# Packed attention and a squared-ReLU MLP on one core: two more banks offered to the folded weights and the second scores, and a new table for the planner

## The chip, the core and the metric

The kernel runs on one core of a Trainium2 chip. TensorE (PE in the profile) multiplies matrices out of SBUF into PSUM, the accumulation memory; PSUM has eight banks, numbered 0 to 7 here, and one bank holds 512 float32 numbers in each of 128 partitions. VectorE (DVE) and ScalarE (ACT) read results from PSUM and write SBUF. GpSimd (POOL) and SyncE (SP) mostly issue DMAs. PEld is TensorE's loading of the stationary operand, which the profile lists as an engine of its own.

The metric is the time of one execution on the device, in microseconds (us); lower is better.

## The reference, cut to what matters

```python
def sm_attn(qq, kk, vv):                       # per batch and head
    a = softmax(qq @ kk.T / 8)
    return a @ vv
p_packed = sm_attn(p, k, v)                    # 32 packed rows
x = sm_attn(q, p_packed, p_packed)             # 576 tokens
h = x.reshape(4608, 512) @ w_in                # heads side by side; w_in is 512 x 2048
out = square(relu(h)) @ w_out                  # w_out is 2048 x 512
```

There are 8 batches of 8 heads, 576 tokens and 64 numbers per head. `x` has 8 x 576 = 4608 rows.

## The kernel before, in words

The work goes batch by batch, eight heads as two "quads" of four. For each batch b, with the names that the code gives to the pieces of work:

- **S1** (L736, for batches 5 to 7 L752): first scores, packed rows times keys. MX (L755) takes the maximum, EX (L763, on ACT) the exponential. E (L769) transposes the exponentials on TensorE, EC copies them out of PSUM (L609 on ACT or L611 on DVE); for batches 5 to 7 a DMA transposes instead.
- **PV** (L783): the packed values. XN (L792) normalizes them, XQ (L796) and XM (L802) turn them, XC copies XM's result.
- **M** (L813, four pieces c of eight matmuls): the *folded weights*. The packed values are multiplied into `w_in`, so that the second attention's probabilities can be multiplied by the result at once and `x` is never formed. A piece fills two banks; MC (L609 or L611) evicts it to SBUF.
- **S2** (L830, for batches 5 to 7 L840): the *second scores*, queries times packed values. A piece of batches 0 to 4 fills part of two banks; SI (L851) takes it out with a transpose, and then follow on DVE and ACT the softmax's maximum (L857), subtraction (L861), exponential (L864, ACT), sum and reciprocal (L867, L868), product (L874) and a transposition into the tile `a` (L878). Batch 0 does this in three parts of 128, 192 and 256 tokens, batch 1 in two of 256 and 320, the others in one.
- **F** (L915 for batches 0 and 1, L887 for the others): hidden layer from `M` and `a`, into two banks; R (L923 or L925, L897 or L899) is the ReLU, Q (L933 or L935, L905 or L907) the square, written into `gT`.
- **Output**: tiles of 128 tokens times `w_out`, F2 (L941). Tiles in the groups of batches 2 to 7 are done instead in pieces GP (L1008) from sums and differences of quarters of `gT` and `w_out` (GS, L993; WS, L986), which saves one product of eight; GC (L1028) adds the pieces up. FZ (L959) is one tile done in two halves. Stores go out on SP, ACT and POOL.

**What sets the order.** No engine's order is written out by hand. `kernel_impl` describes every piece of work to a `Plan` (L47) with `add`: its engine or a choice of engines with a duration for each, the pieces it depends on, a level, and what it takes. `Plan.forward` (L70) is a list scheduler. It walks through its own model of time, and at each step lets go the ready piece of the lowest rank. The rank is the level plus a number from `TABLE` (the dictionary "o", 837 entries), and a second dictionary ("l", 584 entries) leans pieces that have a choice towards ACT or away from it. `run` (L199) then emits the instructions in the order of the planned starts. So every instruction's place on its queue and the choice of ACT or DVE come from the table. Where the plan leaves TensorE idle for long before the first F2, `fills` (L213) puts in idle matmuls (`keep_clock`, L613, on bank 7; L615 in the profile).

**PSUM in the plan.** A piece that writes PSUM names what it takes as a list of alternatives:

```python
PAIRS = [(0, 1), (2, 3), (4, 5)]
ONES = [(4,), (5,), (6,), (7,)]
OUTS = [(6,), (7,)]
RS = [(8 + i,) for i in range(NR)]
```

M, S2, F and S1 take from `PAIRS`, one pair or two. E and PV take from `ONES`. F2 takes from `ONES` (the first tiles) or `OUTS`, and GP and FZ from `OUTS`. `units` (L103) goes through the alternatives in their order and takes the first that is free in the plan; when none is free, the piece isn't ready. A pair is free again when the piece that evicts it is done. The last two banks, 6 and 7, were in `OUTS` and `ONES` alone. The dependencies between instructions that the chip waits for are made afterwards, when the pieces are emitted, from what the instructions read and write.

Of the kernel before, what the change touches and what calls it, by code (L numbers as in the profile page):

```python
# [14 lines left out]
P = 128  # L15
# [26 lines left out]
class Plan:  # L42
# [185 lines left out]
TABLE = {'o': {'Lk.0.0i': -36.900503, 'Lk.0.1i': 0.41924, 'Lk.0.0': -16.56608, 'LP.0': 169.009326, 'Lk.0.1':  # L228
# [292 lines left out]
def kernel_impl(tc, q, k, v, p, w_in, w_out, out):  # L521
# [23 lines left out]
    with ExitStack() as ctx:  # L545
# [42 lines left out]
        M = many("M", 2, [P, NQD, DFF], BF16)  # L588
# [532 lines left out]
        def lasts(b):  # L1121
            if b in PARTS:
                return [f"F.{b}.{x}.{NFB // parts(b)[x][1] - 1}" for x in range(len(parts(b)))]
            return [f"F1.{b}.{NFB - 1}"]
# [275 lines left out]
```

## Time and profile before

| | |
|---|---|
| median of 3 runs | 233.85 us (233.79 to 234.32) |
| the profiled execution | 233.42 us |
| its span, first to last instruction or DMA | 231.7 us |
| what lies around the span | 1.72 us |
| mean granted TensorE clock | 0.994 |
| DVE busy | 199.4 us (86%) |
| ACT busy | 148.4 us (64%) |
| POOL busy | 60.5 us (26%) |

The span counts from the first instruction. A view in stretches gives the busy time of each engine between two moments; the timeline gives instructions in order of time, joined where equal ones follow each other, with the idle time before them and what ended it in brackets; the chain of waits goes back from the last instruction through what released each step. A row "PE L887 MATMUL ... x20" covers twenty matmuls from the start of the first to the end of the last, and matmuls overlap: one lasts longer than the step from one to the next.

### The profile page before, as it was taken

How to read it: one execution, taken by the hardware profiler on the slowest of the kernel's cores; microseconds unless marked ns; L12 is line 12 of the kernel's file. 1: busy time of each engine (PE TensorE's matmuls, PEld its weight loads, DVE VectorE, ACT ScalarE, POOL GpSimd, SP SyncE). 2: the span in 40 equal slices, each digit the busy share in tenths (PEclk: the TensorE clock that was granted, in tenths of full speed). 3: DMA queues.
4: the chain of work that ended last, by engine and by line, in shares of the span. 5: the costliest groups of instructions: out<-in, count | busy, mean ns of one | idle time of the engine just before them, and what ended most of it. 6: DMA issues, size and time to landing. Idle time of an engine off the chain costs nothing.

```text
span 231.7 us, 6374 instructions
## 1 busy us (share of the span) xinstructions
PE 220.0 (95%) x2613; PEld 160.0 (69%) x2630; DVE 199.4 (86%) x336; ACT 148.4 (64%) x243; POOL 60.5 (26%) x108
## 2 busy tenths in 40 slices
PE   8978899999999999999999999999999999999991
PEld 5655664456654476768777877787668888888880
DVE  3679978999989999999999899999999997958340
ACT  3324994268955899775997936859988988310100
POOL 9787646333243575640000000000000000000010
PEclk9999999999999999999999999999999999999997
DMA  7999999999999999999999659757041001515325
GB/s 235 188 161 180 184 204 205 203 193 251 241 229 223 223 219 195 158 148 126 177 193 166 135 94 207 149 83 172 0 96 43 4 0 35 113 36 114 70 52 174
DMA packets 46668, 34.06 MB, mean 147 GB/s; under 512 B 25376, under 2 KB 38368, under 8 KB 46640
## 3 DMA queue, kind: packets, MB, share of 16 engines
q0 software_dynamic: 19488, 18.09, 50.5%
q1 hardware_dynamic: 26304, 14.98, 31.4%
q10 hardware_dynamic: 848, 0.59, 0.9%
q8 instruction: 20, 0.33, 0.6%
q14 instruction: 8, 0.07, 0.1%
HBM read 37.22 MB, written 9.44 MB: 201 GB/s over the span
## 4 chain that ended last, share of the span: by engine, by line
PE 83%; DVE 6%; DMA 5%; POOL 1%; issue 1%; ACT 1%; DVEq 0%; ACTq 0%; POOLq 0%
PE ps L1008 32%; PE ps L887 21%; PE ps L941 15%; PE ps L915 4%; PE ps L813 3%; DMA v_b<-in_v_dram 3%; DMA kq_b<-in_q_dram 2%; PE ps L959 2%; DVE gT L935 1%; PE ps L783 1%; PE ps L830 1%; PE ps L736 1%; PE ps L769 1%; POOL v_b L624 1%; DVE qT L700 1%
## 5 line engine op out<-in xcount | busy, mean ns | idle before, releaser
L897 ACT ACTIVATE r_b<-ps 128x576 bf16<-128x576 f32 x86 | 50.4, 663 | 10.1 <-PE ps L887 9.7
L887 PE MATMUL ps<-a,M 128*128 128x288 bf16 x384 | 52.3, 286 | 0.2 <-issue 0.2
L887 PEld LDWEIGHTS <-M 128*128 128x128 bf16 x384 | 37.3, 98 | 11.1 <-issue 0.2
L941 PE MATMUL ps<-w_out_b,gT 128*128 128x512 bf16 x159 | 41.3, 380 | 1.1 <-issue 0.6
L1008 PEld LDWEIGHTS <-gT 128*128 128x128 bf16 x384 | 36.9, 98 | 7.3 <-issue 1.3
L609 ACT CAST M<-ps 128x1024 bf16<-128x1024 f32 (+1 forms) x30 | 26.9, 933 | 12.4 <-PE ps L813 12.3
L609 ACT COPY o_sb<-ps 128x512 f32<-128x512 f32 (+1 forms) x23 | 12.9, 568 | 32.2 <-PE ps L1008 18.4
L1008 PEld LDWEIGHTS <-gS 128*128 128x128 bf16 x288 | 27.8, 98 | 4.5 <-issue 0.7
L953 POOL DMA_DIRECT2D out_dram<-o_sb x3 | 1.7, 556 | 108.8 <-ACT o_sb L609 103.6
L1028 DVE TENSOR_TENSOR o_sb<-o_sb,ps 128x512 f32<-128x512 f32 x30 | 20.3, 676 | 10.1 <-PE ps L1008 10.0
L907 DVE TENSOR_TENSOR gT<-r_b 128x1152 bf16<-128x1152 bf16 x37 | 27.1, 746 | 1.6 <-ACT r_b L897 1.6
L941 PEld LDWEIGHTS <-gT 128*128 128x128 bf16 x176 | 16.2, 98 | 15.4 <-issue 2.1
L1008 PE MATMUL ps<-wS,gT 128*128 128x256 bf16 x192 | 24.0, 273 | 0.0
L1008 PE MATMUL ps<-w_out_b,gT 128*128 128x256 bf16 x192 | 23.5, 273 | 0.0
L1008 PE MATMUL ps<-wS,gS 128*128 128x256 bf16 x192 | 23.3, 273 | 0.0
L923 ACT ACTIVATE r_b<-ps 128x512 bf16<-128x512 f32 (+2 forms) x30 | 17.8, 659 | 4.8 <-PE ps L915 4.7
L915 PE MATMUL ps<-a,M 128*128 128x256 bf16 (+3 forms) x160 | 18.3, 262 | 2.2 <-DVE a L878 1.0
L915 PEld LDWEIGHTS <-M 128*128 128x128 bf16 x160 | 14.0, 97 | 6.8 <-issue 2.2
L763 ACT ACTIVATE e<-ps,n 128x576 bf16<-128x576 f32 x16 | 11.7, 737 | 7.8 <-DVE n L755 7.6
L615 PE MATMUL ps<-o_sb 128*128 128x256 bf16 x89 | 13.9, 319 | 1.1 <-DVE o_sb L618 1.1
L755 DVE TENSOR_REDUCE n<-ps 128x1 f32<-128x576 f32 x16 | 11.6, 748 | 3.1 <-PE ps L736 3.0
L864 ACT ACTIVATE e<-s 128x1152 bf16<-128x1152 f32 (+4 forms) x11 | 10.0, 912 | 6.2 <-DVE s L861 6.1
(77 smaller groups left out, 322.0 us busy)
## 6 DMA issues: line engine op xcount, KB each, us to landing
out_dram<-o_sb SPq DMA_DIRECT2D x65, 128.0 KB, 3.5
kq_b<-in_k_dram POOLq DMA_DIRECT2D x14, 288.0 KB, 11.1
kq_b<-in_q_dram POOLq DMA_DIRECT2D x10, 288.0 KB, 8.7
w_in_b<-in_moe_w_in_dram POOLq DMA_DIRECT2D x16, 128.0 KB, 5.7
w_out_b<-in_moe_w_out_dram POOLq DMA_DIRECT2D x8, 256.0 KB, 9.6
v_b<-in_v_dram POOLq DMA_DIRECT2D x5, 320.0 KB, 11.8
v_b<-in_v_dram POOLq DMA_DIRECT2D x12, 128.0 KB, 8.7
v_b<-in_v_dram POOLq DMA_DIRECT2D x5, 256.0 KB, 12.2
```

The lines of the kernel that those rows point to most:

```text
L609: nc.scalar.copy(dst, src)
L615: nc.tensor.matmul(half(7)[:, :2 * P], lhsT=zero[:, :P], rhs=zero, start=True, stop=True)
L755: nc.vector.tensor_reduce(n1[b % 2][:, qd:qd + 1], ps1[b, qd], axis=AX.XY if b in XBAR else AX.X, op=ALU.max, negate=True)
L763: nc.scalar.activation(e_out(qd) if b in XBAR else e1[:, qd, :S], ps1[b, qd], ACT.Exp, bias=n1[b % 2][:, qd:qd + 1], accum_out=d1[b % 2][: ...
L887: nc.tensor.matmul(t[:, c], lhsT=M[b % 2][:, qd, fb * FB:(fb + 1) * FB], rhs=a2[b % 2][:, qd, c * HALF:(c + 1) * HALF], start=(qd == 0), s ...
L897: nc.scalar.activation(dst, src, ACT.Relu)
L907: eng.tensor_tensor(out=dst, in0=r, in1=r, op=ALU.mult)
L915: nc.tensor.matmul(t[:, c, m * w:(m + 1) * w], lhsT=M[b % 2][:, qd, fb * FB:(fb + 1) * FB], rhs=a2[b % 2][:, qd, o:o + w], start=(qd == 0) ...
L923: nc.scalar.activation(dst, ph["h", b, x, j], ACT.Relu)
L941: nc.tensor.matmul(po[t], lhsT=gT[:, fb, n0:n0 + P], rhs=w_out_b[:, fb, :], start=(fb == 0), stop=(fb == NFB - 1))
L1008: nc.tensor.matmul(pz[g, k][:, i], lhsT=a[:, f, i * P:(i + 1) * P], rhs=w[:, f], start=(k not in ON and h == 0 and f == 0 and i == 0), sto ...
L1028: nc.vector.tensor_tensor(out=oC(g, i, j), in0=oC(g, *src), in1=pz[g, z], op=ALU.add)
```

## The change

M's pieces and S2's pieces of batches 0 to 4 may also take banks 6 and 7 as a pair, the last alternative in their lists. The table is replaced: all 837 entries of "o" have new values, and "l" has 554 entries in place of 584. Nothing else is edited.

```diff
-TABLE = {'o': {'Lk.0.0i': -36.900503, 'Lk.0.1i': 0.41924, 'Lk.0.0': -16.56608, 'LP.0': 169.009326, 'Lk.0.1':
+TABLE = {'o': {'Lk.0.0i': -2.825591, 'Lk.0.1i': 2.561464, 'Lk.0.0': 25.82095, 'LP.0': 1.735445, 'Lk.0.1': 18.929428,
...
             for c in range(NWC):
                 add(f"M.{b}.{c}", [("PE", 0.216, lambda u, b=b, c=c: m_mm(b, c, u))], [f"XC.{b}"] + [f"LWI.{c}.{i}.{qd}" for i in range(2) for qd in QDS]
-                    + (lasts(b - 2) if b > 1 else []), line="M", take=[PAIRS], mode=3, level=L + 3)
+                    + (lasts(b - 2) if b > 1 else []), line="M", take=[PAIRS + [(6, 7)]], mode=3, level=L + 3)
...
-                add(f"S2.{b}.{x}", [("PE", 0.00088 * tok, lambda u, b=b, x=x: s2_mm(b, x, u))], [f"XQ.{b}"] + tq, line="S2", take=[PAIRS], mode=1, level=l2)
+                add(f"S2.{b}.{x}", [("PE", 0.00088 * tok, lambda u, b=b, x=x: s2_mm(b, x, u))], [f"XQ.{b}"] + tq, line="S2", take=[PAIRS + [(6, 7)]], mode=1, level=l2)
```

The new table is three lines shorter, so a line of the kernel after stands three lower than the same line before; line numbers here are those of the kernel before.

What the edit makes of the program can be read from the two lists of instructions, engine by engine:

| | before | after |
|---|---|---|
| matmuls, idle ones among them | 2632, 89 | 2630, 87 |
| changes of TensorE's tile shape from one matmul to the next, from the first 192-token F on | 64 | 68 |
| e evicted on DVE, on ACT | 7, 3 | 5, 5 |
| M evicted on DVE, on ACT, pieces of 1024 | 4, 24 | 2, 26 |
| ReLU of L887's results on DVE, on ACT | 10, 86 | 5, 91 |
| squares of these on DVE, on ACT | 37, 11 | 43, 5 |
| matmuls of M and S2 into banks 6 and 7 | 0 | 0 |

577 rows, old and new, of the table TABLE are left out of this document.

## The prediction

> **What bounds the kernel now.** I read the page's first part, then a view in five stretches, TensorE's own waits, and the chain of waits at its end.
>
> ```profile
> span 231.7 us, 6374 instructions
> PE 220.0 (95%) x2613; PEld 160.0 (69%) x2630; DVE 199.4 (86%) x336; ACT 148.4 (64%) x243; POOL 60.5 (26%) x108
> ```
> ```profile
> 0.00:23.53 23.53, 19.34 (x257) 13.20 (x258) 15.73 (x42) 8.69 (x16) 19.25 (x38) 1.00 1.07 190
> 23.53:31.43 7.90, 7.13 (x72) 5.62 (x71) 7.64 (x18) 7.71 (x15) 4.44 (x7) 1.00 1.18 192
> 31.43:63.55 32.12, 31.41 (x313) 17.87 (x318) 28.74 (x59) 21.28 (x39) 12.80 (x21) 1.00 1.21 217
> 63.55:197.81 134.26, 133.27 (x1711) 97.75 (x1723) 130.47 (x196) 107.43 (x170) 22.33 (x40) 1.00 0.80 134
> 197.81:231.70 33.89, 28.82 (x265) 25.57 (x262) 16.85 (x26) 3.30 (x7) 1.67 (x3) 0.96 0.37 90
> ```
> ```profile
> PE ps L915 <- DVE a L878: 1.0, 2, 0.6
> PE ps L915 <- ACT r_b L923: 0.5, 2, 0.3
> PE ps L915 <- DVE M L611: 0.3, 1, 0.3
> PE ps L736 <- DVE kT L703: 0.2, 1, 0.2
> ```
> ```profile
> 197.81 19.21 PE ps L1008 x176
> 224.89 1.76 PE ps L959 x16
> 226.67 0.37 ACT o_sb L609
> ```
>
> The stretches' columns are length, then PE, PEld, DVE, ACT and POOL busy, granted clock and DMA. From 31.43 to 197.81 TensorE is idle for 0.71 + 0.99 us out of 166, although DVE is nearly as full. In the last stretch it runs on to 226.65, and one eviction and the last store follow. So from 31.43 on the time is TensorE's amount of work, and an order can give back only what TensorE waits. The waits are early: of those listed, all but the 0.2 us on `kT` are before 31.43. In 23.53:31.43 ACT is busy for 7.71 of 7.90 us and DVE for 7.64: there the evictions are the bound.
>
> **The change part by part.**
>
> *The two banks.* In the new program's list of instructions no matmul of M (L813) or of the second scores (L830) writes bank 6 or 7, as in the old. Whenever the plan let such a piece go, one of the first three pairs was free. That edit costs and gives nothing, and no wait on these banks is added. What is left is the new order: TensorE's work is the same but for two idle matmuls fewer, and the choices of ACT or DVE that the table of the change counts.
>
> *The opening.* Up to the first 192-token F both lists have the same work on TensorE (idle matmuls apart). But both copies of the transposed exponentials (EC of batch 0), and one of ppT, move from DVE to ACT, where they stand between two exponentials.
>
> ```profile
> L609 ACT COPY e<-ps 128x640 bf16<-128x640 bf16 x3 | 2.1, 699 | 0.3 <-PE ps L769 0.3
> L611 DVE COPY e<-ps 128x640 bf16<-128x640 bf16 x7 | 3.3, 486 | 0.9 <-PE ps L769 0.7
> ```
> ```profile
> 9.93 0.45 PE L769 MATMUL ps<-ident,e 128*128 128x128 bf16 x5
> 10.84 0.74 ACT L763 ACTIVATE e<-ps,n 128x576 bf16<-128x576 f32 x1 [1.41 <-DVE n L755]
> 12.22 0.49 DVE L611 COPY e<-ps 128x640 bf16<-128x640 bf16 x1 [0.35 <-PE ps L769]
> 12.76 0.48 PE L783 MATMUL ps<-v_b,e 128*32 128x64 bf16 x40 [0.25 <-DMA w_in_b<-in_moe_w_in_dram]
> 16.48 0.65 DVE L700 STREAM_TRANSPOSE qT<-kq_b 128x448 f32<-128x448 f32 x1 [0.35 <-DMA kq_b<-in_q_dram]
> 23.10 0.38 DVE L878 STREAM_TRANSPOSE a<-n 128x192 f32<-128x192 f32 x1
> 23.53 2.69 PE L915 MATMUL ps<-a,M 128*128 128x192 bf16 x32 [0.64 <-DVE a L878]
> ```
>
> The first transpose ends at 10.38; ACT copies from 10.42 to 11.12, so the second exponential starts at 11.05 in place of 10.84 (+0.21), and its copy takes 0.699 in place of 0.486 (+0.21): PV starts 0.42 later, at 13.18, and so do the second scores. DVE has two copies less, though, and the new list puts a transposition of the queries ahead of the maximum. At 16.48 DVE waited 0.35 us for queries that come by DMA, in the same order in both lists. Laid end to end from PV, DVE gets there at 16.5: the delay is gone in that wait. The DVE work from there to `a` of the second part (L878 at 23.10) is the same set in a slightly better order: 23.0, and F starts at 23.45, 0.1 early. What hides the ACT copies is that 0.35 us; without it F comes about 0.4 late.
>
> *From 23.5 to the first scores of batch 1.*
>
> ```profile
> 26.89 1.08 PE L915 MATMUL ps<-a,M 128*128 128x256 bf16 x8 [0.29 <-ACT r_b L923]
> 28.26 1.91 PE L915 MATMUL ps<-a,M 128*128 128x256 bf16 x16 [0.28 <-DVE M L611]
> 30.00 0.49 PE L615 MATMUL ps<-o_sb 128*128 128x256 bf16 x3
> 30.69 0.60 PE L915 MATMUL ps<-a,M 128*128 128x256 bf16 x4 [0.19 <-ACT r_b L923]
> 31.43 0.70 PE L736 MATMUL ps<-kT,pT 32*32 32x512 bf16 x32
> ```
> ```profile
> L923 ACT ACTIVATE r_b<-ps 128x768 bf16<-128x768 f32 x4 | 3.0, 813 | 0.0
> L923 ACT ACTIVATE r_b<-ps 128x512 bf16<-128x512 f32 x18 | 10.0, 603 | 3.7 <-PE ps L915 3.6
> L933 ACT ACTIVATE gT<-r_b 128x512 bf16<-128x512 bf16 x8 | 4.7, 630 | 0.1
> ```
>
> The old order waits three times and puts in three idle matmuls. The new one mixes the parts (256, 128, 256, 192, 256 tokens in place of 28 matmuls of 256) and needs no idle ones. But every F piece takes a pair that a ReLU must free, and S1 takes two. ACT's list from the first wide ReLU, at 24.3, to the one that frees S1's second pair is three ReLUs of 768, four of 512, an M of 512 and squares of 768, 512 and 512: 2.44 + 2.41 + 0.6 + 0.87 + 1.26 = 7.6 us (0.87 is an estimate from the row of 512 by width), less 0.65 for ten overlaps, so to 31.25, and S1 starts there, 0.2 earlier than at 31.43. By then TensorE has done 2.84 us of F in place of 3.05, at 0.109 us per 256 columns (the chain's 19.21 for 176 matmuls of that width). Early by 0.2 with 0.2 more left is **0.0**. The bounds are -1.25 (the three waits, 0.76, and the idle matmuls, 0.49, all go) and +0.4 (the opening's cover fails).
>
> *More changes of tile shape.* From the first 192-token F on the new list changes the tile shape of TensorE 68 times in place of 64; all four are before the scores of batch 2, around M and S2.
>
> ```profile
> 95.22 0.77 PE ps L813 x24
> 95.99 3.60 PE ps L1008 x32
> 103.72 0.34 PE ps L813 x8
> ```
> ```profile
> L1008 PE MATMUL ps<-wS,gT 128*128 128x256 bf16 x192 | 24.0, 273 | 0.0
> ```
>
> In the chain of waits eight matmuls of L813 take 0.34 and 24 take 0.77, so each further eight cost 0.215, and 0.125 of the first 0.34 is the way in. The 32 of L1008 take 3.60 where 32 x 0.109 is 3.49: 0.11 on the way back. Four at 0.1 to 0.12 are **+0.4**, between 0 (the kinds differ, and some may be cheaper) and 0.5. The Trainium skill speaks against such an order: TensorEngine Tiling (Array Packing), Tiling Modes, Key Properties, says that changing the tiling mode drains the engine. If each drain cost the whole tail of a matmul, 0.273 us of duration less its 0.109 us step, four would be 0.66 by the page's rule; the rows here, 0.11 to 0.125, show less, and I take them.
>
> *F of batch 1 sooner.* The new list puts F of batch 1's first part after 25 output matmuls where the old has 36, and its third piece behind the transposition of the *second* part of `a` (the tile's parts overlap in address order, so it waits for it).
>
> ```profile
> 42.68 1.45 DVE L851 STREAM_TRANSPOSE s<-ps 128x512 f32<-128x512 f32 x2 [0.35 <-PE ps L830]
> 50.90 1.43 DVE L703 STREAM_TRANSPOSE kT<-kq_b 128x576 f32<-128x576 f32 x2
> 54.47 0.68 DVE L925 TENSOR_SCALAR r_b<-ps 128x512 bf16<-128x512 f32 x1
> 56.46 0.51 DVE L878 STREAM_TRANSPOSE a<-n 128x320 f32<-128x320 f32 x1
> 80.07 1.08 PE ps L941 x5
> ```
>
> From 42.68 to that transposition's end at 56.97 DVE spent 14.3 us. The new list has 3.2 us less in between (two `kT`, one ReLU in return for one eviction, one square, three weight sums at about 0.63, less stalls of 0.5 where steps now follow the one they need), and starts at about 41.7: ready at about 52.9. TensorE at its steps (0.216 for L941) arrives at 52.6: a wait of **+0.35**, between 0 and 0.8 (the 0.64 of 23.53 is the nearest row, and the chain may be 0.2 longer). Behind it stand all later matmuls.
>
> *Waits that go.* The 0.2 on `kT`, where the new order has ten transposes and thirteen output matmuls between the scores of batches 2 and 3, and perhaps 0.1 ahead of the former: **-0.3**, between -0.4 and 0. Later DVE and ACT have about 1 us less work each by the counts, and no wait of TensorE on them is seen in the old; I put 0 there, up to +0.5 as each of the listed single waits is 0.2 to 0.6. The end is unchanged: the same last tile, eviction and store.
>
> The sum is 0.0 + 0.4 + 0.35 - 0.3 = **+0.45**: a span of 232.15. With the 1.72 us that the profiled execution has around its span (233.42 - 231.7) it is 233.87, and as that execution was 0.43 below the median of 233.85, a median of **234.3**.
>
> **The rivals.**
> - *The opening unblocks* (faster). If the mixed F pieces keep ACT and DVE ahead, the three waits and the idle matmuls go: -1.25 in place of 0.0, so -0.8, 233.05. For it: DVE and ACT have parts of three widths to choose from, and the list has no idle matmuls there. Against it: ACT is 98% busy in 23.53:31.43, and the list still gives it squares ahead of ReLUs that free pairs.
> - *The ACT copies come through* (slower). If batch 0's queries land before DVE comes for them, or the copies run over their 0.7, the 0.42 is not hidden and everything behind is late: 234.7. It decides at DVE's second 448-wide transposition: later than 16.9, and the rival holds. For it: three more ACT steps in a chain without slack. Against it: the 0.35 us wait on the DMA.
> - *The order is worth nothing.* The bank pair is not used, and crossings and waits cancel: 233.85, give or take 0.3. For it: TensorE has 98 to 99% busy after 31.43 in the old order and the same work in the new. Against it: every extra crossing has a row.
>
> **How the numbers follow.** A measurement of this kernel can tell about 0.3%, 0.7 us, from no change: below 233.15 is faster, above 234.55 slower. The forecast has a chance of 0.45 (233.8 to 234.9: 0.31 of it within 0.3%, 0.14 above); the opening unblocked 0.27 (0.23 below 233.15, the rest within); the ACT copies 0.16, all slower; the order worth nothing 0.12, all within. That is faster 0.23, same 0.47, slower 0.30. The range takes in both outer rivals and the unknowns' ends next to them: 232.9 (the first rival without one of the crossings' 0.1) to 235.2 (the second with 0.5 of later waits).
>
> **What would show it.** Banks 6 and 7 with L813 or L830 in them would make the first step wrong. DVE's second 448-wide transposition at 16.5 and F at 23.45 show the opening; S1 of batch 1 (L736) at 31.2 shows the second step, at 30.3 the first rival. A wait of L915 on L878 near 53 shows the third piece; the scores of batch 2 at about 63.7 with 84 output matmuls done in place of 87 show the sum to there. After it TensorE's idle time must stay below 1.5 us to 226; idle time there on ACT or DVE would make the prediction wrong.

## The result and the profile after

| | before | after |
|---|---|---|
| median of 15 runs each | 233.83 us (232.60 to 236.03) | 235.11 us (233.96 to 236.55) |
| ratio, 95% interval | | 1.0051 (1.0028 to 1.0074) |
| the profiled execution, its span | 233.42, 231.7 us | 235.40, 233.6 us |

The changed kernel is slower by 1.3 us, where +0.45 was forecast. The two profiled executions differ by 2.0 us. Lines of the changed kernel stand three lower (L912 is L915 of before); in the kernels of the experiments, but for e5 and e6, they stand as in the kernel before.

A view in stretches of the changed kernel, with the columns as before. Its borders are the same pieces of work that bound the stretches of the prediction: the first 192-token F, the first scores of batches 1 and 2, and then the first F of batch 3 (106.62 in the kernel before).

```profile
0.00:23.89 23.89, 18.93 (x258) 13.01 (x259) 14.84 (x39) 10.21 (x19) 18.62 (x37) 1.00 1.06 188
23.89:32.09 8.20, 6.52 (x76) 5.25 (x74) 7.68 (x16) 7.82 (x14) 5.80 (x9) 1.00 1.24 203
32.09:64.61 32.52, 31.85 (x307) 17.32 (x311) 29.97 (x60) 21.52 (x37) 12.70 (x21) 1.00 1.20 217
64.61:108.59 43.98, 43.19 (x664) 27.68 (x671) 42.26 (x67) 34.32 (x54) 21.11 (x39) 1.00 1.27 196
108.59:233.60 125.01, 119.81 (x1316) 95.95 (x1317) 105.24 (x156) 75.25 (x123) 1.69 (x3) 1.00 0.53 98
```

The same view of the kernel before, cut at 63.55 and 106.62:

```profile
63.55:106.62 43.07, 42.29 (x660) 27.38 (x667) 41.88 (x66) 32.37 (x52) 21.78 (x39) 1.00 1.22 196
106.62:231.70 125.08, 119.81 (x1316) 95.95 (x1317) 105.44 (x156) 78.35 (x124) 2.21 (x4) 0.99 0.54 101
```

The second to fourth stretch are longer: 8.20 for 7.90, 32.52 for 32.12, 43.98 for 43.07 us. The last is not (125.01, 125.08), and behind 106 us both orders have the same amount of TensorE work left. Work also moves over the borders. The new order leaves 0.21 us more of F for the third stretch (the prediction's 3.05 less 2.84) and three output matmuls, 0.65 us, more for the fourth. At equal work each loss is the stretch's extra length, less what was moved into the stretch, plus what was moved out of it: 0.30 + 0.21 = **0.51**, 0.40 - 0.21 + 0.65 = **0.84**, and 0.91 - 0.65 = **0.26**, together 1.61 us.

What TensorE waits for in the second stretch is in its timeline:

```profile
23.89 2.60 PE L912 MATMUL ps<-a,M 128*128 128x192 bf16 x32
27.47 1.05 PE L912 MATMUL ps<-a,M 128*128 128x256 bf16 x8 [0.63 <-DVE a L875]
28.84 1.72 PE L912 MATMUL ps<-a,M 128*128 128x128 bf16 x20 [0.33 <-DVE M L608]
30.91 0.60 PE L912 MATMUL ps<-a,M 128*128 128x256 bf16 x4 [0.35 <-ACT r_b L920]
32.09 0.70 PE L733 MATMUL ps<-kT,pT 32*32 32x512 bf16 x32 [0.38 <-DVE r_b L922]
```

Four waits stand here, 1.69 us; the old order had three, 0.76 us, and three idle matmuls. Three of the new ones end with DVE: the last transposition of `a` of batch 0, an eviction of M (L608), and a ReLU that the new table gives to DVE (L922) and whose PSUM pair the scores need. That last ReLU had itself waited for ACT, so the two engines hold each other up here:

```profile
31.08 0.96 DVE L922 TENSOR_SCALAR r_b<-ps 128x768 bf16<-128x768 f32 x1 [0.35 <-ACT r_b L920]
```

In the third stretch is the wait that the prediction named:

```profile
53.31 0.27 PE L912 MATMUL ps<-a,M 128*128 128x256 bf16 x1
53.76 1.36 PE L912 MATMUL ps<-a,M 128*128 128x256 bf16 x11 [0.17 <-DVE a L875]
```

The view counts idle time from the modelled end of the matmul before (0.27 us long). A step is the time from the start of one matmul to the start of the next. At the step of 256 columns 0.109 us would have passed from 53.31 to the next start, and 0.45 did: 0.34 us were lost.

### The profile page after: what moved, and what is told of

It reads as the page before. It is cut to its first block, busy times and chain, and to the rows that moved or that the text cites. A ratio compares the mean times of both kernels' runs of the same rounds, so it can differ in the third digit from the quotient of the medians.

```text
span 233.6 us, 6381 instructions
## 1 busy us (share of the span) xinstructions
PE 220.3 (94%) x2612; PEld 159.2 (68%) x2628; DVE 200.0 (86%) x334; ACT 149.1 (64%) x245; POOL 59.9 (26%) x107
## 4 chain that ended last, share of the span: by engine, by line
PE 69%; DVE 11%; DMA 10%; issue 3%; ACT 3%; POOL 1%; SPq 1%; DVEq 0%; ACTq 0%; POOLq 0%
PE ps L1005 23%; PE ps L884 20%; PE ps L938 12%; PE ps L912 5%; PE ps L810 3%; DMA v_b<-in_v_dram 3%; DMA w_in_b<-in_moe_w_in_dram 3%; DMA kq_b<-in_q_dram 2%; DMA out_dram<-o_sb 2%; DVE n L871 2%; PE ps L956 2%; DVE t L864 1%; PE ps L766 1%; PE ps L733 1%; PE ps L827 1%
## 5 line engine op out<-in xcount | busy, mean ns | idle before, releaser
L894 ACT ACTIVATE r_b<-ps 128x576 bf16<-128x576 f32 x91 | 52.4, 658 | 14.7 <-PE ps L884 11.9
L938 PE MATMUL ps<-w_out_b,gT 128*128 128x512 bf16 x160 | 41.4, 380 | 1.4 <-issue 1.0
L606 ACT CAST M<-ps 128x1024 bf16<-128x1024 f32 (+1 forms) x32 | 28.5, 940 | 9.7 <-PE ps L810 8.4
L904 DVE TENSOR_TENSOR gT<-r_b 128x1152 bf16<-128x1152 bf16 x43 | 31.4, 749 | 3.4 <-ACT r_b L894 3.2
L950 POOL DMA_DIRECT2D out_dram<-o_sb x2 | 1.1, 570 | 112.1 <-DVE o_sb L1025 110.9
L938 PEld LDWEIGHTS <-gT 128*128 128x128 bf16 x176 | 15.9, 98 | 16.1 <-issue 1.8
L912 PE MATMUL ps<-a,M 128*128 128x256 bf16 (+3 forms) x160 | 18.4, 262 | 1.9 <-DVE a L875 1.1
L912 PEld LDWEIGHTS <-M 128*128 128x128 bf16 x160 | 13.7, 98 | 6.6 <-issue 1.3
L920 ACT ACTIVATE r_b<-ps 128x512 bf16<-128x512 f32 (+2 forms) x26 | 15.6, 649 | 2.1 <-PE ps L912 1.1
L612 PE MATMUL ps<-o_sb 128*128 128x256 bf16 x87 | 12.8, 308 | 1.1 <-DVE o_sb L615 1.1
```

The lines of the kernel that those rows point to most:

```text
L606: nc.scalar.copy(dst, src)
L612: nc.tensor.matmul(half(7)[:, :2 * P], lhsT=zero[:, :P], rhs=zero, start=True, stop=True)
L894: nc.scalar.activation(dst, src, ACT.Relu)
L904: eng.tensor_tensor(out=dst, in0=r, in1=r, op=ALU.mult)
L912: nc.tensor.matmul(t[:, c, m * w:(m + 1) * w], lhsT=M[b % 2][:, qd, fb * FB:(fb + 1) * FB], rhs=a2[b % 2][:, qd, o:o + w], start=(qd == 0) ...
L920: nc.scalar.activation(dst, ph["h", b, x, j], ACT.Relu)
```

## Experiments

Times are medians beside those of the kernel before on the same chip. Theory after the result: the loss is made between the first 192-token F and 106 us, by changes of tile shape, by that one wait, and by DVE's order ahead of the scores of batch 1. Rivals: the opening, or the later part, where ACT has taken over evictions.

### e1 to e4: whose order, up to where

Each kernel has both tables and plans with both. Every piece that the first plan starts before a cut takes its place and engine from the first plan, all others from the second, and a third pass of the planner lets each engine take its pieces in that order.

```diff
         out, T = self.forward()
+        first = {p.name: (p.start, p.alt) for p in out}
+        self.table = TABLE2
+        out, T = self.forward()
+        self.force = {p.name: first[p.name] if first[p.name][0] < CUT else (1000.0 + p.start, p.alt) for p in out}
+        out, T = self.forward()
```

(CUT stands for a time of the plan: 23.2 us in e1 and e2, 106.5 in e3, 107.2 in e4.)

*e1*: old order up to the first 192-token F, then new.

> Old order and engines for every piece that the old plan starts ahead of the first 192-token F, the new order and engines for all others. Theory (the loss is mostly between the first 192-token F and the time near 106 us: two more trips to tiled matmuls, F's wait for a transposition, late pairs near 31 us): about 1.0 us above the kernel before, ratio 1.004, and the scores of batch 2 (L736) still about 1.3 us of work late. Rival (the opening is the loss: DVE stands before the first 448-wide transposition of queries, or ACT's copies): within 0.2 us of the kernel before, ratio 1.000.

*e2*: new, then old, same cut.

> New order and engines ahead of the first 192-token F, the old order for all others. Theory: 0.3 us above the kernel before (ratio 1.001), with the first 192-token F up to 0.4 us later behind the first pair of batch 0 scores. Rival (opening): 1.2 us above, ratio 1.005.

*e3*: old up to 106 us, then new.

> Old order and engines up to 106 us (the first F of batch 3), the new from there on. Theory: within 0.3 us of the kernel before, ratio 1.000 to 1.001. Rival (the new order loses late, where ACT has taken over work from DVE): 1.2 us above, ratio 1.005.

*e4*: new up to 106 us, then old.

> New order and engines up to 106 us, the old from there on. Theory: as the changed kernel, 1.2 us above the kernel before, ratio 1.005. Rival (late loss): within 0.3 us of the kernel before.

| | opening | up to 106 us | rest | us | ratio, 95% interval |
|---|---|---|---|---|---|
| before | old | old | old | 233.89 | 1 |
| e1 | old | new | new | 234.94 | 1.0059 (1.0037 to 1.0082) |
| e2 | new | old | old | 234.19 | 1.0024 (1.0002 to 1.0046) |
| e3 | old | old | new | 233.65 | 0.9994 (0.9980 to 1.0009) |
| e4 | new | new | old | 235.31 | 1.0064 (1.0047 to 1.0081) |

The part between decides; the theory holds and both rivals fall as the main cause. With the new middle the old opening (e1) isn't better than the new one (after: 1.0051), and the new rest costs nothing behind an old middle (e3). Opening and middle together are 235.31 - 233.65 = 1.66 us (e4 less e3), beside the 1.61 by stretches.

Inside the middle, the stretch from the scores of batch 1 to those of batch 2 goes with its own order: 63.75 - 31.22 = 32.53 us in e1, for 32.52 in the changed kernel, and 64.23 - 32.04 = 32.19 in e2, near the old 32.12. The stretch ahead of that one doesn't. From the first 192-token F to the scores of batch 1 it takes 8.11 us in e1 and 8.30 in e2, so the old order is slow there too when the opening is new. Both have a wait inside the 192-token F that neither whole order has, first e1, then e2:

```profile
24.85 1.28 PE L915 MATMUL ps<-a,M 128*128 128x192 bf16 x16 [0.25 <-DVE M L611]
```
```profile
25.55 1.28 PE L915 MATMUL ps<-a,M 128*128 128x192 bf16 x16 [0.31 <-DVE M L611]
```

Of the loss before the scores of batch 1, these hybrids therefore can't say how much belongs to the opening and how much to the order behind it.

The opening of e2 costs something between nothing and 0.5%. Its timeline shows why one execution is a poor guide there. These are DVE's two 448-wide transpositions of queries in three runs, first the changed kernel, then e3 and e1, which have the old opening:

```profile
15.61 0.65 DVE L697 STREAM_TRANSPOSE qT<-kq_b 128x448 f32<-128x448 f32 x1 [1.07 <-DMA kq_b<-in_q_dram]
16.94 0.64 DVE L697 STREAM_TRANSPOSE qT<-kq_b 128x448 f32<-128x448 f32 x1
```
```profile
14.90 0.65 DVE L700 STREAM_TRANSPOSE qT<-kq_b 128x448 f32<-128x448 f32 x1
16.94 0.65 DVE L700 STREAM_TRANSPOSE qT<-kq_b 128x448 f32<-128x448 f32 x1 [1.09 <-DMA kq_b<-in_q_dram]
```
```profile
15.21 0.64 DVE L700 STREAM_TRANSPOSE qT<-kq_b 128x448 f32<-128x448 f32 x1
16.07 0.63 DVE L700 STREAM_TRANSPOSE qT<-kq_b 128x448 f32<-128x448 f32 x1
```

One list of instructions, up to there, waits 1.09 us for the queries in e3, nothing in e1, and 0.35 in the profile before. The first 192-token F starts at 23.53 (before), 23.99 (e3) and 23.11 (e1) in the old opening, and at 23.89 (after), 23.74 (e2) and 23.85 (e4) in the new. Over all profiles here it is 23.11 to 24.16 in seven with the old opening and 23.69 to 24.16 in six with the new one.

### e5 and e6: the price of a change of tile shape

An idle matmul of 32 columns goes ahead of the first matmul of each output tile and each GP accumulation, 29 in all: in e5 with the tile shape 32*32, in e6 with 128*128. In the order in which the matmuls are issued e6 adds no change, and e5 adds 52: 131 in the whole program in place of 79. The expectation counted 58, two for each. But six of the 29 stand right behind a matmul of a smaller shape (M, PV or a second score), where a change stood already, and add one each.

```diff
+        def turn(bank):
+            nc.tensor.matmul(half(bank)[:32, :32], lhsT=ident[:32, :32], rhs=ident[:32, :32], start=True, stop=True)
...
                 po[t] = half(u[0])
+                turn(u[0])
```

> The kernel before, with an idle matmul of tile shape 32*32 (32 columns) ahead of the first matmul of each output tile (11) and of each GP accumulation (18): 58 more changes of tile shape, order of the work as before. Theory (each change costs TensorE about 0.1 us whatever stands beside it): 58 x 0.093 to 0.1 = 5.4 to 5.8 us and up to 1 us for the 29 matmuls, so 239 to 240.5 us, ratio 1.023 to 1.029. Rival (a change waits for the whole tail of the matmul before, 0.273 less 0.109 us): 9.5 us, 243. Rival (a change between matmuls that are ready costs nothing): as the next kernel.

> As the kernel above, but the 29 idle matmuls have the whole-array shape 128*128 (32 columns too): no more changes than the kernel before. All theories: the 29 matmuls alone, 0.4 us by the 0.109 us that 256 columns take, at most 1.6 us at the 0.056 us of the transposes: 234.3 to 235.5, ratio 1.002 to 1.007.

e5 took 239.76 us (1.0247, 1.0216 to 1.0278), e6 234.45 (1.0033, 1.0007 to 1.0058). The difference is 5.31 us, **0.10 us for one of 52 changes**. The timeline shows the same without a median, first e5 (the idle matmul is L938, GP is L1014), then e6:

```profile
203.62 0.18 PE L938 MATMUL ps<-ident 32*32 32x32 bf16 x1
203.74 1.92 PE L1014 MATMUL ps<-w_out_b,gT 128*128 128x256 bf16 x16
205.59 0.18 PE L938 MATMUL ps<-ident 32*32 32x32 bf16 x1
```
```profile
203.98 1.91 PE L1014 MATMUL ps<-wS,gT 128*128 128x256 bf16 x16
205.72 0.18 PE L938 MATMUL ps<-ident 128*128 128x32 bf16 x1
205.75 1.91 PE L1014 MATMUL ps<-wS,gS 128*128 128x256 bf16 x16
```

From one 32*32 matmul to the next, over sixteen GP matmuls, e5 takes 1.97 us; e6 takes 1.77 from the first GP matmul to the one behind the idle one. The 0.20 is a way out of the whole-array shape and a way back, and each is 0.09 to 0.11: from the idle matmul to the GP behind it 0.12 for 0.03, and from the first GP to the idle matmul 1.85 for 1.74. The view shows no wait for another engine there. The Trainium skill, TensorEngine Tiling (Array Packing), Tiling Modes, Key Properties, says that a change of tiling mode drains the engine. The trace agrees that there is a fixed cost, but the rival in which each change waits for the whole rest of a matmul is out: 9.5 us were expected of it (8.5 with 52 changes). What the tenth is made of stays open. In e6 the weights of the idle matmul are loaded ahead of it, under the matmul before; in e5 the record of that load begins with the idle matmul itself. So the cost can be a load of 0.09 us that is no longer hidden, a drain, or both, and no run here parts them:

```profile
203.62 0.09 PEld L938 LDWEIGHTS <-ident 32*32 32x32 bf16 x1 [0.21 <-issue]
```
```profile
205.62 0.10 PEld L938 LDWEIGHTS <-ident 128*128 128x128 bf16 x1
```

### e7 and e8: banks 6 and 7 used

With the new table the list of instructions is the same without the new option, and with the old table it is the same with it: no plan ever takes the pair. So two pieces of M of batch 0 are put there by hand, in the new order (e7) and the old (e8); order and engines stay.

```diff
         out, T = self.forward()
+        for p in out:
+            if p.name in ('M.0.2', 'M.0.3'):
+                p.take = [[192]]
...
```

(192 stands for banks 6 and 7.)

> The changed kernel with its own order and engines, but the third and fourth piece of M of batch 0 write banks 6 and 7, so that F of batch 0 has all three pairs. Theory (what is late between 23.5 and 32 us is DVE's and ACT's chain, not the pairs): the scores of batch 1 (L736) within 0.15 us of where they are, 8.2 us after the first 192-token F, and the ratio stays at 1.005. Rival (F waits for pairs, and the option would pay if the order used it): the scores 0.4 us or more earlier, ratio 1.003.

> The kernel before with the same two pieces of M in banks 6 and 7. Theory: 0.0 to -0.3 us, as one wait of 0.29 us of F for a ReLU (26.89) may go; ratio 0.999 to 1.000. Rival (pairs): all three waits of F for pairs go, -0.5 us, ratio 0.998.

e7: 234.82 us, 1.0047 (1.0027 to 1.0068). From the first 192-token F to the scores of batch 1 it takes 8.19 us, as without:

```profile
23.69 2.60 PE L915 MATMUL ps<-a,M 128*128 128x192 bf16 x32 [0.57 <-DVE a L878]
27.26 1.05 PE L915 MATMUL ps<-a,M 128*128 128x256 bf16 x8 [0.63 <-DVE a L878]
...
31.88 0.70 PE L736 MATMUL ps<-kT,pT 32*32 32x512 bf16 x32 [0.37 <-DVE r_b L925]
```

The first wait is the same one, on `a`, so a third pair for F was not what was short. The last is the same too, a ReLU that frees a pair for the scores, and the two banks don't reach it. e8: 233.53 us, 0.9984 (0.9957 to 1.0012). By its time alone that is undecided. In its trace the stretch takes 31.71 - 24.01 = 7.70 in place of 7.90 us:

```profile
24.01 2.68 PE L915 MATMUL ps<-a,M 128*128 128x192 bf16 x32 [0.69 <-DVE a L878]
27.23 3.19 PE L915 MATMUL ps<-a,M 128*128 128x256 bf16 x24 [0.20 <-DVE a L878]
30.97 0.60 PE L915 MATMUL ps<-a,M 128*128 128x256 bf16 x4 [0.22 <-ACT r_b L923]
31.71 0.70 PE L736 MATMUL ps<-kT,pT 32*32 32x512 bf16 x32
```

The old waits of 0.29 and 0.28 are gone, and one of 0.20 on `a` stands in their place; the three idle matmuls remain. By the trace the pair is worth some 0.2 us here (7.90 in both the kernel before and e3, 7.70 in e8 and again in e11), and only where it is taken.

### e9: is the gap at 53 us a wait?

```diff
+        moved = {'F2.5.0': 52.231}
```

One output matmul of the new order goes from behind F's third to fifth piece of batch 1 to ahead of them.

> The changed kernel with one output matmul (0.216 us) moved from behind the third to fifth F of batch 1's first part to ahead of them. Theory (F there waits 0.34 us for the transposition of the second part of a): the wait falls to about 0.12, and the stretch between the scores of batches 1 and 2 from 32.52 to 32.31 us; the ratio 0.001 lower than the changed kernel's. Rival (the gap isn't a wait on DVE): 32.52 as before.

234.94 us, 1.0047 (1.0026 to 1.0068); by the time it can't be told from the changed kernel. In its trace the sixteen F matmuls now follow without a gap, and the stretch between the scores is 64.65 - 32.36 = 32.29 us, for 32.52 in the changed kernel and 32.51 in e4:

```profile
50.89 3.07 PE L941 MATMUL ps<-w_out_b,gT 128*128 128x512 bf16 x13
53.79 2.02 PE L915 MATMUL ps<-a,M 128*128 128x256 bf16 x16
```

The wait was real; 0.216 us of work beneath it cost nothing. The rest of it, some 0.1 us, now stands ahead of the sixteen: thirteen output matmuls take 2.81 us at their step of 0.216, and F starts 2.90 after the first.

### e10: DVE's order ahead of the scores of batch 1

```diff
+        moved = {'Q.0.1.0': 26.32}
```

> The changed kernel with the first 768-wide square of batch 0 (L932 at 25.61) moved behind the last transposition of a of batch 0 (L875 at 26.96). Theory (DVE's order makes F's third part late, but the three r_b buffers hold the stage as a whole): F of 256 tokens starts 0.4 us earlier after the first 192-token F (3.2 in place of 3.58), the scores of batch 1 no earlier than 8.2 us after it; ratio 1.005 or higher. Rival (that wait of 0.63 us is the whole loss of the stage): scores 0.4 us earlier, ratio 1.003.

235.98 us, 1.0111 (1.0072 to 1.0150). F of 256 tokens does start earlier, 27.12 - 23.96 = 3.16 us after the first 192-token F, for 3.58. But the scores start 8.77 us after it:

```profile
23.96 2.60 PE L915 MATMUL ps<-a,M 128*128 128x192 bf16 x32 [0.57 <-DVE a L878]
27.12 0.61 PE L915 MATMUL ps<-a,M 128*128 128x256 bf16 x4 [0.21 <-ACT r_b L923]
28.24 0.60 PE L915 MATMUL ps<-a,M 128*128 128x256 bf16 x4 [0.51 <-ACT r_b L923]
29.30 1.90 PE L915 MATMUL ps<-a,M 128*128 128x128 bf16 x20 [0.47 <-DVE M L611]
31.61 0.60 PE L915 MATMUL ps<-a,M 128*128 128x256 bf16 x4 [0.41 <-ACT r_b L923]
32.73 0.70 PE L736 MATMUL ps<-kT,pT 32*32 32x512 bf16 x32 [0.30 <-DVE r_b L925]
```

The wait on `a` (0.63) is gone, and waits for ReLUs take its place (0.21, 0.51, 0.41). That fits the three `r_b` buffers, which a square must free before the next ReLU, but a fourth buffer was not tried, so the buffers as the cause are argued and not shown. Shown is that this wait can be removed without any gain.

### e11: e3, the two banks and one more move, together

e3, with e8's banks, and with one second score of batch 3 moved next to the other (`first['S2.3.0'] = (91.19, ...)`).

> Old order up to 106 us, new order behind, two pieces of M of batch 0 in banks 6 and 7, and the two second scores of batch 3 put side by side (two changes of tile shape less; 74 in the program in place of 79). Theory: -0.2 for the banks, 5 x 0.093 = -0.46 for the changes, up to +0.3 for waits behind 145 us: 233.3 to 233.6, ratio 0.997 to 0.999. Rival (the parts don't add up): ratio 1.000.

233.17 us, 0.9973 (0.9956 to 0.9990), the fastest here and faster than both kernels. The sum of the expectation counted five changes of tile shape less. There are four: scores of batches 5 to 7 have M's tile shape, so a step between these two isn't one. The measured -0.6 us is the large end of what was expected. Which of the three parts paid the times don't say, as e3 and e8 alone can't be told from the kernel before; the trace has the 0.2 us of the banks (31.45 - 23.75 = 7.70 us) and four changes less.

## Why the prediction was right or wrong

The time, 235.11, lies in the range (232.9 to 235.2), at its very end; the likeliest case, within 0.3%, did not come. That the range holds it is luck: its upper end was made of ACT's copies coming through and of 0.5 us of later waits on ACT or DVE, and the loss came in the main from neither. By its steps:

- **The two banks**: right. No matmul of M or S2 uses them, and e7 and e8 show what it would be worth.
- **The opening**: PV came 0.37 us later behind the scores (3.45 to 3.82 us; 0.42 forecast). That the wait on the queries hides this was wrong as a fixed fact: that wait is anything from 0 to 1.1 us for one order. F started at 23.89, not 23.45. The second rival was to be told by the second 448-wide transposition later than 16.9; it was at 16.94, but in e3 too, with the copies on DVE, so that sign told nothing. What the opening costs, at most 0.5% in e2, isn't settled closer.
- **From 23.5 to the first scores of batch 1**: wrong, +0.5 in place of 0.0. The step laid ACT's list end to end, to 31.25 (the scores 7.8 us behind an F at 23.45), and left out DVE, though the stretch's row had DVE busy for 7.64 of 7.90 us. The new table gives the ReLU that frees the scores' second pair to DVE, and it ended at 31.08 + 0.96 = 32.04. 8.20 was measured, in the changed kernel and in e4 and e9 alike, and DVE ends three of the four waits. How much of the 0.5 the new opening brings about is open (e2: 8.30 with the old order).
- **Changes of tile shape**: right, 0.4 us for four: e5 and e6 give 0.10 for one, though their changes were miscounted beforehand. Not all are before the scores of batch 2, though: four are there, two more before 106 us, two fewer behind. With the wait of 0.34 the four make 0.74 of the 0.84 us that the third stretch lost.
- **F of batch 1 sooner**: right, 0.34 for 0.35 (e9).
- **Waits that go, -0.3**: wrong, and a misreading. The quoted 0.2 us on `kT` is not between batches 2 and 3. It is at 9.31 us, in the opening, where the timeline of the kernel before shows it; the changed kernel has it too (0.25 at 8.61):

```profile
9.31 0.69 PE L736 MATMUL ps<-kT,pT 32*32 32x512 bf16 x16 [0.25 <-DVE kT L703]
```

The gap that I had put it to, ahead of the scores of batch 3, is a lost record. The list has one output matmul between the transposes and the scores of batch 3. The trace of before doesn't have it, that of e6 does, where the same order was profiled again:

```profile
66.85 0.44 PE L769 MATMUL ps<-ident,e 128*128 128x128 bf16 x5
67.43 0.70 PE L736 MATMUL ps<-kT,pT 32*32 32x512 bf16 x32
```
```profile
66.61 0.44 PE L769 MATMUL ps<-ident,e 128*128 128x128 bf16 x5
66.89 0.38 PE L945 MATMUL ps<-w_out_b,gT 128*128 128x512 bf16 x1
67.20 0.70 PE L736 MATMUL ps<-kT,pT 32*32 32x512 bf16 x32
```

From transposes to scores it is 0.58 and 0.59 us in the two: nobody waited, and nothing could go. In its place this part lost 0.26 us, of which two changes of tile shape are 0.2.

- **Later waits, the end**: right; behind 106 us the two orders take the same time (e3).

With +0.5 for 0.0 and +0.26 for -0.3, the sum 0.45 becomes 0.45 + 0.5 + 0.56 = 1.5 us, beside a measured 1.3 (medians) and 1.66 (e4 less e3).

## What to carry to other kernels

Where a stretch has two engines nearly full, lay out both lists, and the places where one waits for the other, before you give it a price; moving one step there traded one wait for another (e10). Before a term is built on a small wait, find that wait's one instruction in the timeline, and count the records against the program's list: a missing matmul looks just like idle time. When an order has been searched as a whole, cut it at points where both orders have done the same work: four hybrids tested here what two traces had only suggested, and showed too where a cut makes a wait that neither order has.

## What the runs showed of the hardware

A change of TensorE's tile shape costs about 0.1 us between whole-array matmuls that wait for nothing else (e5 less e6). If each costs the same, an estimate, the 64 changes behind the first 192-token F of the kernel before are some 6 us of 233, more than the 1.7 us that TensorE is idle from 31.43 to 197.81. And TensorE's steps repeat from run to run: the stretch between the scores of batches 1 and 2 took 32.12 us in the kernel before and in e3, 32.52 in the changed kernel and 32.51 in e4. The queries of batch 0, one of the first loads, held DVE until 16.94 in e3 and no longer than 16.07 in e1, which has the same list of instructions up to there: a difference of 0.9 us or more.
